# Moving the next batch's first scores and the up-projection heads by one chunk, and all whole down-projection blocks to Strassen, in an attention-plus-MLP kernel

## The chip, the cores and the metric

One core of a Trainium2 chip. The metric is the device time of one execution in microseconds (us). Kernels sent together run on the same chip, beside runs of the kernel before.

## The reference, cut to what matters

```python
# attention, batch 8, S = 3008, D = 256, d_qk = 64
attn = np.maximum(scale * (z @ z.T), 0.0) ** 2      # symmetric; no softmax
x    = u * (attn @ v)
# MLP over all 24064 tokens, d_ff = 2048
h = x @ w_in
g = h / (1 + np.exp(-1.702 * h))
out = g @ w_out
```

## The kernel before: the parts that matter

Each batch goes through six chunks of 512 query rows (the last has 448). TensorE (PE) does everything that is large. A *score unit* (two 64-row matmuls, a ReLU on ACT, a square on DVE) is taken ahead of the chunk that needs it, between attention matmuls ("hosted"). As the scores are symmetric, most units are also turned by a DMA transpose on SP's queue and used a second time (`tt`). Attention chunks run with the array as two 64-row halves; chunk 5, the up-projection and the Strassen products use the full array.

```python
def attend(b, i, both=False):
    ...
    half = [(0, TOP, NJ - 1), (1, LOW, NJ - 1)]           # the last 64 keys
    elif i == NCH - 1:                                     # full array: half block FIRST
        order = [half] + [[(c, FULL, j)] for c in cs for j in js]
    else:                                                  # 64-row halves, swapped in the middle
        order = [[(0, TOP, j), (1, LOW, j)] for j in js] + [half] + [[(1, TOP, j), (0, LOW, j)] for j in js]
    ...
    acc, turn = {}, NJ if order[-1][0][1] != FULL else -1
    def step(k):
        ...
            if k == turn:
                behind(acc["sig"], ins)                    # waits for the no-op
        if k == turn - 1:
            acc["sig"] = post(done)                        # sig = pool.nop(), after these matmuls
```

In the middle of a 64-row chunk the two halves swap accumulator banks, and `post`/`behind` keeps their order by a no-op on POOL: PE waits for POOL, POOL for PE.

```python
def load_w(k):                       # up weights W1 in 4 loads (2 MB of f32), down weights W2 in 4
    if k == 0:
        pool.tensor_copy(hold, XT[0, 1][:, 0, :1])
    if k < 4: pool.dma_start(W1[...], ...)
    else:     pool.dma_start(W2[...], ...)

LAGY = 2 * NFG + 4                   # up groups hosted by chunk 5: 20
NST = 4                              # blocks 0..3 by Strassen (7 products), the others:
def down64(b, k): ...                # 64-row halves, hosts the next batch's first 12 score units
# (chunk, step): which load; all in batch 0
LOADW = {(3, NJ + 1): 0, (3, NJ + 11): 1, (4, 2): 2, (4, 10): 3, (5, 0): 4, ...}
```

## Time and profile before

| | before |
|---|---|
| time, median | 1203.2 us (1201.6 to 1206.8, 4 runs) |
| span of the profiled run | 1200.5 us |
| least matmul time (below) | 1178.0 us |
| span above that | 22.5 us |

The page of the kernel before: busy time by engine, then the chain of waits.

```profile
PE 1189.5 (99%) x11775; PEld 720.5 (60%) x11775; DVE 828.1 (69%) x1273; ACT 766.4 (64%) x899; POOL 306.3 (26%) x363
...
PE 95%; DMA 2%; DVE 2%; ACT 1%; issue 0%; ACTq 0%
PE o L322 37%; PE hg L363 27%; PE st L463 18%; PE yp L529 8%; PE sc L226 6%; DMA tt<-a 2%; DVE a L254 1%; ACT rl L240 0%; PE w L97 0%; DVE gt L372 0%; DVE zst L122 0%; ACT gf L371 0%; DVE s L436 0%; DVE s L434 0%; DVE ZT L139 0%
```

So PE is the bound. Here `o` is attention, `hg` the up-projection, `st` a Strassen product, `yp` the plain down-projection, `sc` scores.

Windows of batch 1 (chunks 0 to 4; chunk 5 with up heads; up-projection with products; 64-row down):

```profile
core 0: us, PE busy (x) PEld busy (x) DVE busy (x) ACT busy (x) POOL busy (x), PEclk, DMA share, GB/s
165.70:223.30 57.60, 57.19 (x536) 29.75 (x532) 29.44 (x43) 29.50 (x34) 6.73 (x11) 1.00 0.90 155
223.30:250.40 27.10, 27.10 (x134) 12.73 (x131) 22.64 (x34) 20.47 (x20) 13.81 (x13) 1.00 0.46 69
250.40:299.50 49.10, 49.10 (x567) 36.06 (x567) 42.10 (x65) 33.00 (x44) 19.52 (x21) 1.00 0.44 127
299.50:313.40 13.90, 13.90 (x242) 11.53 (x240) 6.63 (x12) 10.42 (x13) 0.78 (x1) 1.00 0.72 150
```

PE idles 0.4 us in 147.7. The DMA engines are 90% busy in chunks 0 to 4 (the transposes).

The timeline of PE at the border from products to the 64-row down-projection, and inside it:

```profile
297.87 1.06 PE L463 MATMUL st<-W,s 128*128 128x128 f16 x16
298.86 0.50 PE L529 MATMUL yp<-W,gt 64*128 64x256 f16 x6
...
300.50 2.35 PE L529 MATMUL yp<-W,gt 64*128 64x256 f16 x40
302.69 0.59 PE L226 MATMUL sc<-ZT 64*128 64x512 f16 x4
```

Read starts, not durations, as matmuls overlap. Forty 64-row matmuls take 302.69 - 300.50 = 2.19 us, 55 ns each. Sixteen products at 55.9 ns would end at 298.76, but the next starts at 298.86: a change of array mode costs 0.10 us.

*Least matmul time.* In undisturbed stretches the spacing of full-array matmuls of N columns is N / 2.4 GHz + 2.5 ns (74 64-row attention matmuls of 512 columns, which run two at a time, take 7.99 us: 215.9 ns a pair; 240 products of 128 columns take 13.41 us: 55.9 ns each). The Trainium skill, "TensorE: Matmul & The Clock Gate", section "Wait — 56ns, not 53.3ns?", gives the same formula, and this trace agrees. I add it up over all matmuls of a stretch and call the rest *excess*.

Two more views, of batch 0, that the change will alter. PE's timeline, and the windows there:

```profile
58.06 0.38 PE L322 MATMUL o<-tt,V 64*128 64x512 f16 x2
58.88 1.04 PE L322 MATMUL o<-tt,V 64*128 64x512 f16 x8 [0.45 <-DMA tt<-a]
```

### The profile page before, as it was taken

The numbers are of one execution on the slowest core, as the hardware profiler recorded it, in microseconds if no ns is written. First come the engines' busy times: TensorE is split into PE (matmuls) and PEld (weight loads), VectorE is DVE, ScalarE is ACT, GpSimd is POOL, SyncE is SP. The second block draws the span as 40 slices with busy tenths as digits, with TensorE's granted clock in tenths as the row PEclk, the third lists the DMA queues.
The fourth block names the chain that finished last, engine by engine and source line by source line (L and its number), as shares of the span: only waits on it lengthen the run. The fifth ranks groups of instructions, "written<-read, shape, count | busy, mean of one in ns | idle before, by whom it ended". The sixth has DMA issues, their size and how long they took to land.

```text
span 1200.5 us, 28209 instructions
## 1 busy us (share of the span) xinstructions
PE 1189.5 (99%) x11775; PEld 720.5 (60%) x11775; DVE 828.1 (69%) x1273; ACT 766.4 (64%) x899; POOL 306.3 (26%) x363
## 2 busy tenths in 40 slices
PE   8999999999999999999999999999999999999998
PEld 3446765467654676546764468554775447855577
DVE  7659955597545976469654696638965489564886
ACT  6767684476844768367683676836677366772764
POOL 5144300352004520044200461015520145101000
PEclk9999999999999999999999999999999999999999
DMA  9987389562994639944399453984449854497012
GB/s 221 190 132 123 121 161 163 87 155 73 162 172 87 151 91 163 165 83 137 94 171 164 77 137 101 184 139 78 137 117 173 142 85 138 120 178 130 1 37 72
DMA packets 370816, 153.38 MB, mean 128 GB/s; under 512 B 317536, under 2 KB 362720, under 8 KB 370688
## 3 DMA queue, kind: packets, MB, share of 16 engines
q1 hardware_dynamic: 334400, 114.99, 49.6%
q0 software_dynamic: 35456, 35.86, 14.6%
q8 instruction: 92, 1.51, 0.5%
q10 hardware_dynamic: 832, 0.72, 0.2%
q14 instruction: 36, 0.29, 0.1%
HBM read 60.29 MB, written 24.64 MB: 71 GB/s over the span
## 4 chain that ended last, share of the span: by engine, by line
PE 95%; DMA 2%; DVE 2%; ACT 1%; issue 0%; ACTq 0%
PE o L322 37%; PE hg L363 27%; PE st L463 18%; PE yp L529 8%; PE sc L226 6%; DMA tt<-a 2%; DVE a L254 1%; ACT rl L240 0%; PE w L97 0%; DVE gt L372 0%; DVE zst L122 0%; ACT gf L371 0%; DVE s L436 0%; DVE s L434 0%; DVE ZT L139 0%
## 5 line engine op out<-in xcount | busy, mean ns | idle before, releaser
L371 ACT ACTIVATE gf<-hg 128x1024 f32<-128x1024 f32 (+1 forms) x384 | 385.8, 1006 | 167.3 <-PE hg L363 140.2
L240 ACT ACTIVATE rl<-sc 128x1024 f16<-128x1024 f32 x307 | 303.9, 1026 | 210.4 <-PE sc L226 208.3
L322 PEld LDWEIGHTS <-V 64*128 64x128 f16 (+1 forms) x4052 | 238.8, 94 | 246.1 <-issue 9.4
L363 PE MATMUL hg<-xt,W 128*128 128x512 f16 (+1 forms) x1408 | 354.6, 374 | 0.1
L372 DVE TENSOR_SCALAR gt<-gf 128x1024 f16<-128x1024 f32 (+1 forms) x384 | 275.8, 718 | 89.1 <-ACT gf L371 85.2
L254 DVE TENSOR_TENSOR a<-rl 128x1024 f16<-128x1024 f16 x272 | 190.0, 701 | 186.2 <-ACT rl L240 184.2
L322 PE MATMUL o<-a,V 64*128 64x512 f16 (+2 forms) x1982 | 313.3, 372 | 0.3 <-DVE a L254 0.3
L191 POOL DMA_DIRECT2D uq<-in_u_dram x188 | 129.4, 695 | 508.7 <-PE sc L226 342.3
L322 PE MATMUL o<-tt,V 64*128 64x512 f16 (+1 forms) x1790 | 218.2, 376 | 1.6 <-DMA tt<-a 1.3
L363 PEld LDWEIGHTS <-W 128*128 128x128 f16 x1536 | 141.2, 98 | 117.5 <-issue 0.3
L463 PEld LDWEIGHTS <-gt 128*128 128x128 f16 x2176 | 132.4, 98 | 28.7
L226 PE MATMUL sc<-ZT 64*128 64x512 f16 (+1 forms) x684 | 120.6, 366 | 4.2 <-DVE ZT L139 2.5
L463 PEld LDWEIGHTS <-s 128*128 128x128 f16 x1632 | 99.2, 98 | 20.7
L176 POOL CAST V<-vst 128x512 f16<-128x512 f32 x96 | 91.2, 986 | 64.2 <-DMA vst<-in_v_dram 64.0
L529 PE MATMUL yp<-W,gt 64*128 64x256 f16 x1664 | 104.0, 269 | 0.0
L529 PEld LDWEIGHTS <-gt 64*128 64x128 f16 x1664 | 80.4, 94 | 19.2 <-POOLq L85 4.1
L339 DVE TENSOR_TENSOR xt<-o,ut 128x512 f16<-128x512 f32 x80 | 51.5, 685 | 38.5 <-PE o L322 38.5
L463 PE MATMUL st<-WT,gt 128*128 128x128 f16 x1088 | 71.9, 219 | 0.0
L463 PE MATMUL st<-W,gt 128*128 128x128 f16 x1088 | 71.7, 219 | 0.0
L463 PE MATMUL st<-WT,s 128*128 128x128 f16 x1088 | 71.5, 219 | 0.0
L473 ACT ACTIVATE uP<-st 128x256 f32<-128x256 f32 x102 | 39.0, 382 | 35.7 <-DVE y L479 30.8
L226 PEld LDWEIGHTS <-ZT 64*128 64x128 f16 x684 | 37.9, 94 | 39.3 <-issue 7.8
(47 smaller groups left out, 626.5 us busy)
## 6 DMA issues: line engine op xcount, KB each, us to landing
vst<-in_v_dram SPq DMA_DIRECT2D x39, 512.0 KB, 5.0
uq<-in_u_dram POOLq DMA_DIRECT2D x156, 128.0 KB, 3.4
out_dram<-y SPq DMA_DIRECT2D x33, 512.0 KB, 3.8
tt<-a SPq DMA_TRANSPOSE x234, 3.4
uq<-in_u_dram POOLq DMA_DIRECT2D x32, 112.0 KB, 2.9
out_dram<-y POOLq DMA_DIRECT2D x7, 512.0 KB, 5.1
vst<-in_v_dram SPq DMA_DIRECT2D x8, 384.0 KB, 4.8
out_dram<-y POOLq DMA_DIRECT2D x7, 384.0 KB, 3.2
```

Source lines behind the costliest of these rows:

```text
L176: pool.tensor_copy(V16[b][:, n0:n0 + VB, k, :].rearrange("p n (q c) -> p n q c", c=QW), vst.rearrange("p n (q k c) -> p n q k c", k=NCC, c ...
L191: eng.dma_start(uq[k * QW:(k + 1) * QW, :n // QW].rearrange("t q k c -> t q (k c)"), src[:, :, cs])
L226: pe.matmul(sc[:, r, :m * P], zt[h, 2 * kp + r, :], zt[h, (qi + 1) * CB - m:(qi + 1) * CB, :], start=True, stop=True,)
L240: act.activation(rl, sc, AF.Relu, scale=csc)
L254: dve.tensor_tensor(a, rl, rl, ALU.mult)
L322: ins = pe.matmul(acc[c][:, :n], V16[b][h, j, c, :], weights(b, i, j)[h], start=(k, m) == first[c], stop=(k, m) == final[c],)
L339: dve.tensor_tensor(x[:, c, :n], acc[c][:, :n], ut[:, :n], ALU.mult)
L363: pe.matmul(hg[:, e, :n], W1[:, c, ff * P:(ff + 1) * P], XT[b, i][:, c, :n], start=(c == 0), stop=(c == NCC - 1),)
L371: act.activation(gf[:, :, :n], hg[:, :, :n], AF.Gelu_apprx_sigmoid, scale=1.0 / FSC)
L372: dve.tensor_scalar(g, gf[:, :, :n], FSC, None, ALU.mult)
L463: pe.matmul(bank[:, m, :], lhs()[:, f, m, :], right[:, ff, :], start=name in ("P1", "P2", "P5") and m == 0 and ff == 0, stop=ff == NFF // ...
L529: ins = pe.matmul(yp[s // per][:, s % per, :], GT[b, k, ff // CB][h, ff % CB, s * P:(s + 1) * P], W2[h, ff, :], start=new, stop=n == last[ ...
```

## The change

Intent: the 64-row down-projection goes; every whole block is done by Strassen (7 products instead of 8). Then something else must host the next batch's first score units: chunk 5 becomes a 64-row chunk and hosts ten of them. The up heads (18 groups now) move to chunk 4, which becomes a full-array chunk, except in the last batch. z of the next batch is loaded in chunk 4. After batch 0, V is cast by the DMA that loads it instead of on POOL, with the two channel halves interleaved, so that V's weight loads have stride 2. One scaling in four after the head moves to ACT. The core of the diff:

```diff
+    def full(b):
+        return NCH - 2 if b < B - 1 else NCH - 1
...
-        elif i == NCH - 1:
-            order = [half] + [[(c, FULL, j)] for c in cs for j in js]
+        elif i == full(b):
+            order = [[(c, FULL, j)] for c in cs for j in js]
+            order.insert(0 if i == NCH - 1 else len(order), half)     # chunk 4: half block LAST
...
-                    acc[c][:, :n], V16[b][h, j, c, :], weights(b, i, j)[h],
+                    acc[c][:, :n], V16[b][h, j].rearrange("p (c k) -> p k c", k=NCC)[:, c], weights(b, i, j)[h],
...
+        if q >= LAGY and q % 4 == 1:
+            act.activation(g, gf[:, :, :n], AF.Copy, scale=FSC)
+        else:
+            dve.tensor_scalar(g, gf[:, :, :n], FSC, None, ALU.mult)
...
-        return NST if b < B - 1 else NCH
+        return NCH - 1 + b % 2
...
-    def down64(b, k):  ...
+    def down(b, k, s):  ...                      # full array, only block 5 of even batches
-    LAGY = 2 * NFG + 4
+    LAGY = 2 * NFG + 2
...
-    LOADW = {(3, NJ + 1): 0, (3, NJ + 11): 1, (4, 2): 2, (4, 10): 3, (5, 0): 4, (5, 6): 5, (5, 12): 6, (5, 18): 7}
+    LOADW = {(2, NJ + 12): 0, (3, 4): 1, (3, 12): 2, (3, 20): 3, (4, 16): 4, (4, 22): 5, (4, 28): 6, (4, 34): 7}
...
+                if more and (i, n) == (NCH - 2, 2):
+                    load_z(b + 1)
```

Cut: larger buffer counts, the deferral of the next batch's transposes to the tail, new schedules of score units (`NEXT` for chunk 5), `load_u` and W1 in the interleaved channel order.

More of the change, by code (lines that the diff above doesn't have):

```diff
@@ L75 @@
     dve.memset(nil, 0.0)
-    late = []
+    late, LATE = [], []
     ZT, V16, UQ, UT, XT, unit, TT = {}, {}, {}, {}, {}, {}, {}
@@ L102, in first_z @@
             ZT[0] = pz.tile([P, NJ, P], F16, name="ZT", tag="ZT")
-            ZT["st"] = [pa.tile([P, CB * CB, 2, DQK], F16, name="zst", tag="tt", bufs=14) for _ in range(2)]
+            ZT["st"] = [pa.tile([P, CB * CB, 2, DQK], F16, name="zst", tag="tt", bufs=15) for _ in range(2)]
             ZT["f"] = [pw.tile([P, CB * CB, DQK], F32, name="zf", tag="y") for _ in range(2)]
@@ L148, in load_z @@
         for n0 in range(0, NJ, NU):
-            zst = pu.tile([P, NU, 2, DQK], F16, name="zst", tag="vst", bufs=3)
+            zst = pu.tile([P, NU, 2, DQK], F16, name="zst", tag="zst")
             full = min(NU, NJ - 1 - n0)
@@ L159, with load_v @@
     VB = 4
-    def load_v(b, n0, eng):
+    def load_v(b, n0):
         if n0 == 0:
-            V16[b] = pz.tile([P, NJ, NCC, P], F16, name="V16", tag="V16")
-        if b or n0 < 3 * VB:
-            vst = pu.tile([P, VB, D], F32, name="vst", tag="vst", bufs=3)
+            V16[b] = pz.tile([P, NJ, D], F16, name="V16", tag="V16")
+        if b:
+            dst, eng = V16[b][:, n0:n0 + VB], pool
         else:
-            vst = pa.tile([P, VB, D], F32, name="vst", tag="tt", bufs=14)
+            dst, eng = pa.tile([P, VB, D], F32, name="vst", tag="tt", bufs=15), sp if n0 else act
         full = min(VB, NJ - 1 - n0)
-        eng.dma_start(vst[:, :full, :], v[b, n0 * P:(n0 + full) * P].rearrange("(n p) c -> p n c", p=P))
+        eng.dma_start(dst[:, :full, :], v[b, n0 * P:(n0 + full) * P].rearrange("(n p) c -> p n c", p=P))
         if full < VB:
             for h in range(2):
-                eng.dma_start(vst[h * SREM:(h + 1) * SREM, full, :], v[b, S0:S])
-        for k in range(NCC):
-            pool.tensor_copy(
-                V16[b][:, n0:n0 + VB, k, :].rearrange("p n (q c) -> p n q c", c=QW),
-                vst.rearrange("p n (q k c) -> p n q k c", k=NCC, c=QW)[:, :, :, k, :],
-            )
+                eng.dma_start(dst[h * SREM:(h + 1) * SREM, full, :], v[b, S0:S])
+        if b == 0:
+            for n in range(0, VB, 2):
+                pool.tensor_copy(V16[b][:, n0 + n:n0 + n + 2], dst[:, n:n + 2])
     def width(i):
@@ L186, in load_u @@
         n = width(i)
-        uq = pu.tile([P, CH // QW, NCC, QW], F32, name="uq", tag="uq")
+        uq = pu.tile([P, CH // QW, QW, NCC], F32, name="uq", tag="uq")
         src = u[b, i * CH:i * CH + n].rearrange("(q t) c -> t q c", t=QW)
@@ L190, in load_u @@
             cs = slice(k * NCC * QW, (k + 1) * NCC * QW)
-            eng.dma_start(uq[k * QW:(k + 1) * QW, :n // QW].rearrange("t q k c -> t q (k c)"), src[:, :, cs])
+            eng.dma_start(uq[k * QW:(k + 1) * QW, :n // QW].rearrange("t q c k -> t q (c k)"), src[:, :, cs])
         UQ[b, i] = uq
@@ L197, in turn_u @@
         UT[b, i] = ut
-        dve.transpose(ut[:, :, :n // QW, :].rearrange("p k q t -> p q k t"), UQ.pop((b, i))[:, :n // QW])
+        dve.transpose(
+            ut[:, :, :n // QW, :].rearrange("p k q t -> p q k t"),
+            UQ.pop((b, i))[:, :n // QW].rearrange("p q c k -> p q k c"),
+        )
     def folded(b, i):
@@ L241, in square @@
         if folded(b, i) and jp == 2 * i:
-            a = pa.tile([P, CB, 2, P], F16, name="a", tag="a", bufs=21)
+            a = pa.tile([P, CB, 2, P], F16, name="a", tag="a", bufs=22)
             unit[b, i, jp] = a
@@ L245, in square @@
             dve.tensor_tensor(a.rearrange("p q r c -> p r q c"), r4, r4, ALU.mult)
-            unit[b, i, jp + 1] = pa.tile([P, 2, 2, CH // 2], F16, name="ad", tag="a", bufs=21)
+            unit[b, i, jp + 1] = pa.tile([P, 2, 2, CH // 2], F16, name="ad", tag="a", bufs=22)
             sp.dma_start_transpose(
@@ L251, in square, with turn_unit @@
             return
-        a = pa.tile([P, 2, CH], F16, name="a", tag="a", bufs=21)
+        a = pa.tile([P, 2, CH], F16, name="a", tag="a", bufs=22)
         unit[b, i, jp] = a
         dve.tensor_tensor(a, rl, rl, ALU.mult)
-        cj = jp // 2
-        if cj > i and (turned(b, i) or cj < NCH - 1):
-            if (b, i, cj) not in TT:
-                TT[b, i, cj] = pa.tile([P, CB, CB, P], F16, name="tt", tag="tt", bufs=14)
-            k0 = 2 * (jp % 2)
-            def turn_it():
-                sp.dma_start_transpose(
-                    TT[b, i, cj][:, k0:k0 + 2].rearrange("p r g c -> p (r g) c"),
-                    a.rearrange("p r c -> p (r c)"),
-                )
-            if b and i == 0 and 6 <= jp < NU - 2:
-                late.append(turn_it)
-                return
-            turn_it()
-            while late and (i, jp) == (1, NU - 1):
-                late.pop(0)()
+        if jp // 2 > i and (turned(b, i) or jp < NU - 2):
+            if b and i == 0 and LATE:
+                late.append(((jp + 2) % NU, lambda: turn_unit(b, i, jp, a)))
+            else:
+                turn_unit(b, i, jp, a)
+    def turn_unit(b, i, jp, a):
+        cj = jp // 2
+        if (b, i, cj) not in TT:
+            TT[b, i, cj] = pa.tile([P, CB, CB, P], F16, name="tt", tag="tt", bufs=15)
+        k0 = 2 * (jp % 2)
+        sp.dma_start_transpose(
+            TT[b, i, cj][:, k0:k0 + 2].rearrange("p r g c -> p (r g) c"),
+            a.rearrange("p r c -> p (r c)"),
+        )
     def weights(b, i, j):
@@ L367, in up_group @@
         if fg % 2 == 0:
-            GT[b, k, fg // 2] = pa.tile([P, CB, CH], F16, name="gt", tag="tt", bufs=14)
+            GT[b, k, fg // 2] = pa.tile([P, CB, CH], F16, name="gt", tag="tt", bufs=15)
         g = GT[b, k, fg // 2][:, (fg % 2) * FFG:(fg % 2 + 1) * FFG, :n]
@@ L371, in up_group @@
         act.activation(gf[:, :, :n], hg[:, :, :n], AF.Gelu_apprx_sigmoid, scale=1.0 / FSC)
-        dve.tensor_scalar(g, gf[:, :, :n], FSC, None, ALU.mult)
-        if SUMS:
-            SUMS.pop(0)()
+        if q >= LAGY and q % 4 == 1:
+            act.activation(g, gf[:, :, :n], AF.Copy, scale=FSC)
+        else:
+            dve.tensor_scalar(g, gf[:, :, :n], FSC, None, ALU.mult)
+        for s_ in [SUMS.pop(0) for _ in range(min(len(SUMS), 1 + (len(SUMS) > 8)))]:
+            s_()
         if k < nst(b) and fg == NFG - 1:
             SUMS.extend(left_sums(b, k) + (weight_sums() if b == k == 0 else []))
-    NST = 4
     def nst(b):
-        return NST if b < B - 1 else NCH
+        return NCH - 1 + b % 2
     SUMS, ST = [], {}
@@ L398, in load_w @@
         if k < 4:
-            w1v = moe_w_in.rearrange("(q k c) f -> q c k f", k=NCC, c=QW)
+            w1v = moe_w_in.rearrange("(q c k) f -> q c k f", k=NCC, c=QW)
             pool.dma_start(W1[k * QW:(k + 1) * QW], w1v[k])
@@ L431, in left_sum @@
             return
-        s_ = ST[b, k, name, h] = pa.tile([P, CB, 2, P], F16, name="s", tag="a", bufs=21)
+        s_ = ST[b, k, name, h] = pa.tile([P, CB, 2, P], F16, name="s", tag="a", bufs=22)
         if name == "S1":
@@ L510, in store, with down @@
                 )
-    def down64(b, k):
-        ns = blocks(b)[k][1] // P
-        shift, per = (2, 2) if ns == CB else (1, 1)
-        order = [(s, (s + shift) % ns, ff) for s in range(ns) for ff in range(NFF)]
-        turns = [32] if ns == CB else [16, 32]
-        last = {s // per: n for n, o in enumerate(order) for s in o[:2]}
-        yp, sigs = {}, {}
-        def step(n):
-            s0, s1, ff = order[n]
-            done = []
-            for s, h in ((s1, LOW), (s0, TOP)):
-                new = s // per not in yp
-                if new:
-                    yp[s // per] = ps1.tile([P, 2, D], F32, name="yp", tag="ps1")
-                ins = pe.matmul(
-                    yp[s // per][:, s % per, :], GT[b, k, ff // CB][h, ff % CB, s * P:(s + 1) * P], W2[h, ff, :],
-                    start=new, stop=n == last[s // per],
-                )
-                if n in turns:
-                    behind(sigs[n], ins)
-                done.append(ins)
-            if n + 1 in turns:
-                sigs[n + 1] = post(done)
-            for m in yp:
-                if n == last[m]:
-                    if (b, k) not in Y:
-                        Y[b, k] = pw.tile([P, CB, D], F32, name="y", tag="y")
-                    act.activation(Y[b, k][:, m * per:(m + 1) * per, :], yp[m][:, :per, :], AF.Copy, scale=1.0 / FSC)
-            if n == len(order) - 1:
-                store(b, k, pool)
-        return turns, [lambda n=n: step(n) for n in range(len(order))]
-    LAGY = 2 * NFG + 4
-    HEAD = 2
+    def down(b, k, s):
+        if s % 2 == 0:
+            ST[b, k, "yp"] = ps1.tile([P, 2, D], F32, name="yp", tag="ps1")
+        yp = ST[b, k, "yp"]
+        for ff in range(NFF):
+            pe.matmul(
+                yp[:, s % 2, :], GT[b, k, ff // CB][:, ff % CB, s * P:(s + 1) * P], W2[:, ff, :],
+                start=s % 2 == 0 and ff == 0, stop=ff == NFF - 1, skip_group_check=True,
+            )
+        last = s == blocks(b)[k][1] // P - 1
+        if s == 0:
+            Y[b, k] = pw.tile([P, CB, D], F32, name="y", tag="y")
+        if s % 2 or last:
+            act.activation(Y[b, k][:, s - s % 2:s + 1, :], yp[:, :s % 2 + 1, :], AF.Copy, scale=1.0 / FSC)
+        if last:
+            store(b, k, pool)
+    LAGY = 2 * NFG + 2
+    HEAD, HEAD0 = 2, 16
     def pieces(b, i):
@@ L559, in pieces @@
         return lst[:k] + lst[-2:] + lst[k:-2]
-    TAIL = {1: {n: 1 for n in (3, 12, 44, 54)}, 2: {n: 1 for n in (4, 25, 34, 43)}}
+    NEXT = {n: 1 for n in (4, 9, 14, 19, 29, 34, 39, 44)} | {NJ: 2}
     SCHED = {
@@ L565 @@
         2: {n: 1 for n in (2, 7, 12, 17)} | {NJ: 2},
-        3: {n: 1 for n in (14, 34)} | {NJ: 2},
-        4: {NJ: 2},
-        5: {},
+        3: {n: 1 for n in (6, 14, 32, 38)} | {NJ: 2},
+        4: {},
+        5: NEXT,
     }
+    SCHED_LAST = SCHED | {3: {n: 1 for n in (14, 34)} | {NJ: 2}, 4: {NJ: 2}, 5: {}}
     TURN0 = {(i, (38, 28)[i] if i < 2 else NJ + 4 if i < NCH - 1 else 12): i for i in range(NCH)}
@@ L575 @@
     TURN = {(1, NJ + 4): 2, (2, NJ + 4): 3, (4, NJ + 4): 4, (5, 8): 5}
-    LOADW = {(3, NJ + 1): 0, (3, NJ + 11): 1, (4, 2): 2, (4, 10): 3, (5, 0): 4, (5, 6): 5, (5, 12): 6, (5, 18): 7}
-    LOAD = {(3, NJ + 4): 4, (4, NJ + 5): 5}
+    LOADW = {(2, NJ + 12): 0, (3, 4): 1, (3, 12): 2, (3, 20): 3, (4, 16): 4, (4, 22): 5, (4, 28): 6, (4, 34): 7}
+    LOAD = {(3, NJ + 20): 4, (4, NJ + 5): 5}
     FIRST_ZT = {7: 3, 19: 4, 27: NCH - 1}
@@ L582 @@
         1: {0: 2, 8: 2, 15: 2, 22: 2, 30: 2, 38: 2},
-        2: {n: 1 for n in (0, 3, 7, 11, 30, 34, 38, 42)} | {NJ: 2},
-        3: {n: 1 for n in (4, 9, 14, 19)} | {NJ: 2},
-        4: {n: 1 for n in (4, 12, 20, 34)} | {NJ: 2},
-        5: {},
+        2: {n: 1 for n in (0, 3, 7, 11, 28, 32, 36, 40, 44)} | {NJ: 2},
+        3: {n: 1 for n in (3, 7, 11, 15, 19, 28, 32, 36, 40)} | {NJ: 2},
+        4: {},
+        5: NEXT,
     }
@@ L601 @@
     first_z(CB, 2 * CB, act)
-    load_v(0, 0, act)
+    load_v(0, 0)
     first_z(2 * CB, 4 * CB, sp)
     for n0 in (VB, 2 * VB):
-        load_v(0, n0, sp)
+        load_v(0, n0)
     first_z(4 * CB, NJ, sp)
     for n0 in range(3 * VB, NJ, VB):
-        load_v(0, n0, sp)
+        load_v(0, n0)
     warm_up(7)
@@ L625 @@
         nup = NCH * NFG
-        sched, turn, load = (SCHED, TURN, LOAD) if b else (SCHED0, TURN0, LOAD0)
-        head = 0
+        more = b + 1 < B
+        sched = SCHED0 if b == 0 else SCHED if more else SCHED_LAST
+        turn, load = (TURN, LOAD) if b else (TURN0, LOAD0)
+        head, first = 0, HEAD0 if b == 0 else HEAD
         for i in range(NCH):
+            host = b + 1 if more and i == NCH - 1 else b
+            if host > b:
+                fill(host)
+                LATE.append(host)
             for n, step in enumerate(attend(b, i, b == 0 and i < 2)):
@@ L641 @@
                     load_w(LOADW[i, n])
-                take(b, sched[i].get(n, 0))
-                if i == NCH - 1 and n >= HEAD and (n - HEAD) * LAGY // (2 * NJ - 2 - HEAD) >= head and head < LAGY:
+                if more and (i, n) == (NCH - 2, 2):
+                    load_z(b + 1)
+                take(host, sched[i].get(n, 0))
+                if i == full(b) and n >= first and (n - first) * LAGY // (2 * NJ - 2 - first) >= head and head < LAGY:
                     up_group(b, head)
@@ L646 @@
                 step()
-        more = b + 1 < B
         if more:
@@ L650 @@
                 load_u(b + 1, i)
-            load_z(b + 1)
             for n0 in range(0, NJ, VB):
-                load_v(b + 1, n0, sp)
-            fill(b + 1)
+                load_v(b + 1, n0)
         prods = products(nst(b))
@@ L662 @@
             product(b, *prods.pop(0))
-        for kp in prods:
-            product(b, *kp)
+        steps = [lambda kp=kp: product(b, *kp) for kp in prods]
+        if nst(b) < NCH:
+            k = NCH - 1
+            steps += [lambda s=s: down(b, k, s) for s in range(blocks(b)[k][1] // P)]
+        late.sort(key=lambda t: t[0])
+        for step in steps:
+            step()
             if SUMS:
                 SUMS.pop(0)()
+            for _, turn_it in [late.pop(0) for _ in range(min(len(late), 1 + (len(steps) < 10)))]:
+                turn_it()
+        LATE.clear()
         if more:
-            for k in range(NST, NCH):
-                turns, steps = down64(b, k)
-                at = {n: 3 - len(turns) for n in turns} | TAIL[len(turns)]
-                for n, step in enumerate(steps):
-                    take(b + 1, at.get(n, 0))
-                    step()
+            while late:
+                late.pop(0)[1]()
+            take(b + 1, 2)
 _INS = ['u', 'v', 'z', 'moe_w_in', 'moe_w_out']
```

## The prediction

> **What bounds the kernel now.** TensorE. The page's first part: PE busy 99% of 1200.5 us, clock 1.0. The chain of waits: 95% PE (attention 37%, up-projection 27%, Strassen products 18%, 64-row down-projection 8%, scores 6%). The waits view shows almost no PE idle. POOL (26%), ACT (64%), DVE (69%) are off the path. Windows of one batch (147.7 us): chunks 0-4 57.6, chunk 5 with up heads 27.1, up-projection with products 49.1, 64-row down 13.9. DMA is 90% busy in chunks 0-4 (transposes).
>
> **The change, costed.**
> 1. Down-projection. In the PE timeline 40 64-row matmuls advance 2.18 us: 54.5 ns each, 128 per whole block = 6.97 us. A Strassen block is 112 matmuls at 55.9 ns (240 in 13.41 us) = 6.25 us. Ten blocks switch (block 4 of seven batches, block 5 of batches 1, 3, 5): -7.2 us. Block 5 of even batches goes from 96 x 54.5 = 5.23 us to 48 full-array matmuls, estimated 109 ns each: no gain.
> 2. Scores, up groups and attention are moved, totals equal. Chunk 4 (full array) hosts 18 up groups; chunk 5 (64-row) ten score units of the next batch: two more mode changes per batch. The Trainium skill, "TensorEngine Tiling (Array Packing)", Key Properties, says a mode change drains the array; here each costs about 0.1 us of start-to-start time. 7 x 2 x 0.1 = +1.5 us.
> 3. In chunk 5 each score unit needs 1026 ns of ACT and gets five attention pairs (0.95 us) plus its own 0.22 us: just enough. Attention tiles are tight (12 for chunk 5, 8 sums, 10 new in 22): estimated 0 to 0.5 us per batch.
> 4. Deferred transposes pile up in the short tail (about 10 us): eight at 2 us each. Chunk 1 may wait: 0 to 1 us per batch.
> 5. V's POOL casts (986 ns each) mostly go; V's weight loads become stride-2. "TensorE: Matmul & The Clock Gate", Weight-path perf modes, allows strided columns for the fast load; no run shows it yet. Loads take 94-98 ns against 189-216 ns per attention slot; even doubled they should hide. Worth nothing.
> 6. DVE gets the sums of ten more Strassen blocks (8 x 0.75 us each), loses eight output scalings a batch to ACT; both have room.
>
> **Sum.** -7.2 + 1.5, perhaps -1 from stalls that vanish and +1 to +2 from new ones: about -6 us.
>
> **Predicted: 1197.5 us, 8 in 10 between 1188 and 1209. Faster by over 2%: 0.04; within 2%: 0.92; slower by over 2%: 0.04.**
>
> **What would show each step.** (1) The 64-row down group gone, products up from 3808 to 4928 at the same spacing, a small full-array down group; batches 0.7 to 1.4 us shorter. (2) About 0.1 us extra at the borders of chunks 4 and 5. (3) PE idle for ACT rl in chunk 5. (4) PE idle for transposed tiles in chunks 0-1. (5) V's weight load near 95 ns, or longer with attention still at 216 ns per pair. (6) No PE hg waits in chunk 4.
>
> **What would make it wrong.** Stride-2 loads so slow that attention's spacing grows (an estimated 471 us of the span is attention columns: 10% is 47 us). Transposed z or V late for chunk 5 or chunk 0. Transposes starving chunk 1. DVE behind in chunk 4 (scaling plus sum 1.48 us per group against about 1.4 us of PE). On the other side, stalls that I took as unavoidable going away.

## More of the kernel before

```profile
core 0: us, PE busy (x) PEld busy (x) DVE busy (x) ACT busy (x) POOL busy (x), PEclk, DMA share, GB/s
57.00:62.00 5.00, 4.55 (x44) 1.93 (x42) 2.50 (x4) 3.83 (x4) 0.73 (x2) 1.00 1.39 183
62.00:67.00 5.00, 5.00 (x50) 2.26 (x48) 3.14 (x4) 0.68 (x2) 2.71 (x5) 1.00 0.93 180
72.00:82.00 10.00, 10.00 (x73) 4.88 (x69) 5.98 (x9) 6.67 (x7) 5.39 (x8) 1.00 1.15 168
```

I read a DMA share over 1 as packets that wait for one another: these stretches are the fullest of the kernel. Yet PE waits only 0.45 us for a transposed tile. The eight weight loads here (W1's four and the first four of W2), by the view of tile W:

```profile
DMA to landing us min/median/max: 4.5/5.4/7.6
```

## The result

| | before | after |
|---|---|---|
| time, median | 1203.2 us | 1220.8 us (1220.6 to 1221.4, 4 runs) |
| ratio | | 1.0143 (95%: 1.012 to 1.0166) |
| span | 1200.5 us | 1218.8 us |
| least matmul time | 1178.0 us | 1170.6 us |
| span above that | 22.5 us | 48.2 us |
| mean granted clock | 1.000 | 0.995 |

Ratios are the mean time of one kernel's fast runs over that of the other's in the same rounds, so not quite the ratio of the medians quoted.

The kernel became slower, and the range 1188 to 1209 missed. But the least matmul time fell by 7.3 us, as predicted (7.2). The gain was there and was more than lost. Where, by batch and chunk (excess in us, from the starts of PE's matmuls in the trace; about 5.3 us of start-up, the same in both kernels, are left out of batch 0):

| excess, us | chunks 0-1 | 2 | 3 | 4 | 5 | up | tail | sum |
|---|---|---|---|---|---|---|---|---|
| batch 0 before | 6.7 | 0.0 | 0.6 | 0.2 | 0.4 | 0.0 | 0.3 | 8.1 |
| batch 0 after | 6.7 | 0.2 | 5.5 | 11.7 | 0.8 | 0.0 | 0.2 | 25.2 |
| batches 1-6 before, mean | 0.2 | 0.2 | 0.0 | 0.2 | 0.1 | 0.0 | 0.2 | 0.85 |
| batches 1-6 after, mean | 0.5 | 0.0 | 0.1 | 0.6 | 0.6 | 0.0 | 0.4 | 2.2 |

Balance: -7.3 (matmul time) + 17.1 (batch 0) + 8.1 (batches 1 to 6) + 0.5 (batch 7) = +18.3 us, the difference of the spans (the parts are rounded).

Page of the changed kernel, the same lines:

```profile
PE 1192.4 (98%) x11423; PEld 721.2 (59%) x11423; DVE 826.9 (68%) x1327; ACT 821.9 (67%) x971; POOL 231.3 (19%) x325
...
PE 85%; DMA 4%; DVE 3%; issue 3%; ACT 2%; POOL 2%; POOLq 0%; ACTq 0%; DVEq 0%
```

"98% busy" hardly moved, yet 48 us lie above the least time: a PE at half clock counts as busy, and short waits vanish in the modelled ends of matmuls. The chain of waits is the better sign: PE's part fell from 95% to 85%.

Windows of batch 1 (chunks 0 to 3; chunk 4; chunk 5; up-projection with products; tail), to be read against the four rows before:

```profile
182.10:229.20 47.10, 47.03 (x438) 24.61 (x434) 27.00 (x40) 29.88 (x33) 4.41 (x6) 1.00 0.96 174
229.20:255.50 26.30, 25.75 (x120) 11.38 (x118) 18.92 (x28) 17.69 (x18) 8.46 (x9) 1.00 0.69 82
255.50:267.30 11.80, 11.62 (x118) 5.97 (x118) 9.56 (x16) 9.67 (x11) 5.13 (x8) 1.00 0.35 80
267.30:319.00 51.70, 51.70 (x586) 37.64 (x585) 39.36 (x66) 41.53 (x54) 11.52 (x16) 1.00 0.43 88
319.00:331.30 12.30, 12.01 (x212) 11.69 (x211) 9.66 (x18) 3.85 (x9) 0.16 (x1) 1.00 0.91 160
```

PE now idles in chunk 4 (0.55 us), chunk 5 and the tail, where it did not before.

The tail of batch 0 (`yp` is now the small full-array form): 48 matmuls in 5.23 us after 0.10 us for the mode change at the end, 109 ns each, as estimated.

```profile
176.31 5.40 PE L524 MATMUL yp<-W,gt 128*128 128x256 f16 x48
181.64 0.61 PE L228 MATMUL sc<-ZT 64*128 64x512 f16 x4
```

Now batch 0. PE's timeline, chunks 3 and 4:

```profile
58.70 0.39 PE L326 MATMUL o<-tt,V 64*128 64x512 f16 x2
62.62 1.04 PE L326 MATMUL o<-tt,V 64*128 64x512 f16 x8 [3.53 <-DMA tt<-a]
63.50 0.66 PE L228 MATMUL sc<-ZT 64*128 64x512 f16 x4
63.94 1.92 PE L326 MATMUL o<-a,V 64*128 64x512 f16 x8
65.65 0.64 PE L228 MATMUL sc<-ZT 64*128 64x512 f16 x2
...
81.92 1.01 PE L326 MATMUL o<-tt,V 128*128 128x512 f16 x2 [5.89 <-DMA tt<-a]
...
89.77 0.38 PE L326 MATMUL o<-a,V 128*128 128x512 f16 x1
92.28 0.39 PE L326 MATMUL o<-a,V 128*128 128x512 f16 x1 [2.13 <-POOLq L85]
```

Three waits, two for transposed tiles and one for POOL's no-op (line 85 is `pool.nop()`). After the first, eight matmuls that should take 0.86 us start to start take 1.71 (63.94 to 65.65). The windows show why:

```profile
57.00:62.00 5.00, 2.10 (x20) 0.88 (x16) 2.51 (x4) 2.83 (x3) 0.00 (x0) 1.00 1.37 126
62.00:67.00 5.00, 4.38 (x28) 1.76 (x30) 1.80 (x3) 2.61 (x3) 0.00 (x0) 0.69 1.03 138
72.00:82.00 10.00, 4.11 (x20) 1.82 (x19) 1.78 (x3) 1.48 (x2) 0.00 (x0) 0.95 1.66 113
82.00:92.00 10.00, 8.15 (x24) 2.88 (x23) 3.06 (x4) 4.09 (x4) 4.37 (x6) 0.71 0.79 93
```

The column PEclk falls to 0.69 and 0.71. The trace's clock records give half clock for 3.41 us from 63.9 and for 6.83 us from 81.0. The Trainium skill, "TensorE: Matmul & The Clock Gate", Part 1, says that about 3.4 us without matmuls brings the clock to half, in free-running windows of 3413 ns. The durations agree, one and two such windows. The threshold does not. I marked off windows of 3.413 us from the clock records of all 13 traces and counted in each how long PE was idle. Leaving out the first 12 us and the last 4, every fall came at the end of a window with 1.96 us or more of idle time (2.13 us before the fall at 63.9), and no window with 1.70 us or less was followed by one; in the first 12 us, 1.4 to 1.5 us was enough in e3, e6 and e9. The wait of 2.1 us that ends at 92.28 did no harm: it lay across the border of two windows at 91.2, with 1.1 us in each. So the place of a wait counts as well as its length. The two long waits here cost an estimated 1.7 and 2.9 us on top of themselves, half of the time that PE then worked at half clock.

Why were the tiles late? W1's four loads in this kernel, the same view as before:

```profile
DMA to landing us min/median/max: 13.5/17.2/18.0
```

And the transposes around them, listed from the trace:

```
                    kernel before                        changed kernel
             issued    landed                     issued    landed
transpose     52.87     58.84  transpose           52.44     62.58
transpose     54.73     59.67  W1, first of four   54.07     67.53
transpose     57.68     62.56  transpose           54.20     76.07
transpose     59.05     63.53  W1, last of four    55.56     73.59
transpose     60.43     66.14  transpose           57.59     81.88
W1, first     60.59     65.13  next batch's z      70.56     83.15
W1, the rest  66.8-67.9 71.5-74.0
```

W1's 2 MB now leave POOL as one burst at 54 us, into the busiest stretch of the kernel. In the program the four loads stand at separate steps from the end of chunk 2 to the middle of chunk 3, but no no-op of POOL's queue stands between them: the trace has the no-op of chunk 2 at 47.05 and that of chunk 3 at 63.70, behind the burst. In the kernel before they stood behind the no-op of chunk 3, which ran at 59.97, and three of them also behind a load of u (64.29 to 66.80). In e2 below, put behind that no-op again, they leave at 61.3. POOL's timeline, the changed kernel first, then the kernel before:

```profile
54.07 1.99 POOL L405 DMA_DIRECT2D W<-in_moe_w_in_dram  x4
```

```profile
60.59 0.54 POOL L400 DMA_DIRECT2D W<-in_moe_w_in_dram  x1 [0.29 <-issue]
```

The transpose issued at 54.20 then takes 22 us to land instead of 5. The Trainium skill, "DMA: Bandwidth & Descriptors", Queues, rings and completion order, says that each DMA engine takes turns between its queues packet by packet; the landings fit that (both queues make progress, both slowly), but no run here shows the order of packets. Sharing alone does not explain it: from 66 to 74 us the DMA engines moved 46 GB/s at a share of 1.26, where the kernel before moved 152 GB/s at 0.82. Why loads and transposes slow one another that much stays open.

The third wait has another source. POOL's timeline in the changed kernel:

```profile
83.97 1.08 POOL L152 DMA_DIRECT2D zst<-in_z_dram  x1
85.05 1.49 POOL L155 DMA_DIRECT2D zst<-in_z_dram  x2
90.96 0.83 POOL L156 COPY zst<-zst 128x768 f16<-128x768 f16 x1 [4.42 <-DMA zst<-in_z_dram]
```

`load_z` puts a copy on POOL that waits for z. PE goes on at 92.28, just after that copy (90.96 + 0.83 = 91.79). The no-op of chunk 4 stands behind the copy; its record is at 92.21. And chunk 4 needs no such no-op. The line `turn = NJ if order[-1][0][1] != FULL else -1` recognises a 64-row chunk by its last step; the change put the half block last in the full-array chunk 4, so the test came out wrong, and a full-array chunk got a half-way synchronisation through POOL. The Trainium skill, "TensorE: Matmul & The Clock Gate", table of specifications, calls GpSimdE's queue strictly first-in first-out; the trace agrees, as the no-op (92.21) comes after the copy that stands before it (90.96).

In batches 1, 3 and 5 the same no-op costs 0.7, 0.9 and 1.05 us, in batch 4 0.2 and in batches 2 and 6 nothing. The trace shows why: it runs 14.5, 13.2, 14.7, 13.9, 14.8 and 13.2 us after the first attention matmul of chunk 4 in batches 1 to 6, and what it costs is what exceeds 13.75 us. In batches 1 to 5 it runs within 0.2 us of the landing of the last z load, so a later z is a longer wait.

### The profile page after: what moved, and what is told of

Read it like the earlier page. It is cut to its first block, busy times and chain, and to the rows that moved or that the text cites. A ratio compares the mean times of both kernels' runs of the same rounds, so it can differ in the third digit from the quotient of the medians.

```text
span 1218.8 us, 27565 instructions
## 1 busy us (share of the span) xinstructions
PE 1192.4 (98%) x11423; PEld 721.2 (59%) x11423; DVE 826.9 (68%) x1327; ACT 821.9 (67%) x971; POOL 231.3 (19%) x325
## 4 chain that ended last, share of the span: by engine, by line
PE 85%; DMA 4%; DVE 3%; issue 3%; ACT 2%; POOL 2%; POOLq 0%; ACTq 0%; DVEq 0%
PE o L326 34%; PE hg L367 22%; PE st L468 21%; PE sc L228 6%; DMA zst<-in_z_dram 3%; PE yp L524 2%; DMA tt<-a 1%; ACT rl L242 1%; DVE a L256 1%; DVE gt L379 1%; ACT gf L375 1%; POOL uq L190 1%; POOL zst L152 1%; DMA ZT<-zst 1%; POOL zst L156 0%
## 5 line engine op out<-in xcount | busy, mean ns | idle before, releaser
L379 DVE TENSOR_SCALAR gt<-gf 128x1024 f16<-128x1024 f32 (+1 forms) x328 | 230.8, 704 | 149.3 <-ACT gf L375 147.4
L326 PE MATMUL o<-a,V 64*128 64x512 f16 (+3 forms) x2272 | 302.9, 369 | 2.5 <-POOLq L85 2.1
L326 PE MATMUL o<-tt,V 64*128 64x512 f16 (+1 forms) x1524 | 236.3, 378 | 11.9 <-DMA tt<-a 9.7
L468 PEld LDWEIGHTS <-gt 128*128 128x128 f16 x2816 | 169.5, 98 | 32.2 <-issue 1.6
L468 PEld LDWEIGHTS <-s 128*128 128x128 f16 x2112 | 127.2, 98 | 22.8
L468 PE MATMUL st<-WT,gt 128*128 128x128 f16 x1408 | 92.9, 219 | 1.1 <-ACT uP L478 1.1
L468 PE MATMUL st<-W,gt 128*128 128x128 f16 x1408 | 92.3, 219 | 0.0
L468 PE MATMUL st<-WT,s 128*128 128x128 f16 x1408 | 91.0, 219 | 0.0
L484 DVE SCALAR_TENSOR_TENSOR y<-st,uP 128x256 f32<-128x256 f32 x132 | 55.5, 420 | 29.4 <-ACT uP L478 18.3
L443 DVE TENSOR_TENSOR s<-gt,s 128x1024 f16<-128x1024 f16 x88 | 59.8, 683 | 0.0
L441 DVE TENSOR_TENSOR s<-s,gt 128x1024 f16<-128x1024 f16 x88 | 59.6, 682 | 0.0
```

What stands on the lines that cost most here:

```text
L326: ins = pe.matmul(acc[c][:, :n], V16[b][h, j].rearrange("p (c k) -> p k c", k=NCC)[:, c], weights(b, i, j)[h], start=(k, m) == first[c], s ...
L379: dve.tensor_scalar(g, gf[:, :, :n], FSC, None, ALU.mult)
L441: dve.tensor_tensor(s_, ST[b, k, "S1", h], a11, ALU.subtract)
L443: dve.tensor_tensor(s_, a12, ST[b, k, "S2", h], ALU.subtract)
L468: pe.matmul(bank[:, m, :], lhs()[:, f, m, :], right[:, ff, :], start=name in ("P1", "P2", "P5") and m == 0 and ff == 0, stop=ff == NFF // ...
L484: dve.scalar_tensor_tensor(y[:, :, o, c], ST[b, k, "bank" + x], 1.0 / FSC, ST[b, k, "after" + u_], ALU.mult, ALU.add,)
```

## The experiments

Theory A: the loss has two main causes in batch 0, W1's early burst (transposes starved, then half clock) and the stray no-op behind z's copy, and small waits in each later batch. Rival: the denser score schedule of batch 0 (11 units in chunk 3 instead of 6) needs more transposes than the queue can turn.

The first four ran on one chip; the kernel before took 1206.6 us there (7 runs).

### e1: without the stray synchronisation

```diff
-        acc, turn = {}, NJ if order[-1][0][1] != FULL else -1
+        acc, turn = {}, NJ if not both and i != full(b) else -1
```

> The changed kernel, with the half-way synchronisation of chunk 4 taken out (a full-array chunk needs none; it is only set because the half block stands last there). Theory A (this sync is a no-op in POOL's queue and waits behind the copy of the next batch's z): the PE waits put down to POOLq vanish, 2.3 us in batch 0 and 0.7, 0.9, 1.05 us in batches 1, 3, 5; time 1220.8 - 5 = about 1216. Rival (something else holds PE there, for example accumulator banks): the same waits come back under another name, time within 1 us of 1220.8.

Measured: 1212.3 us (1208.7 to 1221.5), ratio 1.0055 (1.0008 to 1.0102); span 1209.5. All POOLq waits in chunk 4 are gone: batches 1 to 6 have 0.12 us of excess in chunk 4. But batch 0's chunk 4 still has 9.4 us: W1's burst still starves the transposes (landings up to 23 us after issue), with waits of 2.1 and 2.6 us, each followed by 3.41 us of half clock. The no-op is confirmed as the cause of its wait; the total is not compared with the changed kernel here, as that ran on another chip (e11 below, the changed kernel on a third chip, has a ratio of 1.006, so the times of e1 and e2 alone show no gain).

### e2: W1 behind the middle of chunk 3

```diff
-    LOADW = {(2, NJ + 12): 0, (3, 4): 1, (3, 12): 2, (3, 20): 3, (4, 16): 4, ...
+    LOADW = {(3, NJ): 0, (3, NJ + 1): 1, (3, NJ + 2): 2, (3, NJ + 3): 3, (4, 16): 4, ...
```

> The changed kernel, with the four loads of the up-projection weights placed behind the middle of chunk 3 of batch 0, about where the kernel before has them, instead of from the end of chunk 2 on. Theory A (these 2 MB, issued as one burst at 54 us, fill the DMA engines, and the transposed tiles that PE needs land up to 20 us late, after which PE runs at half clock): the 3.7 and 6.05 us waits and the 5 us lost at half clock go; batch 0 shrinks by about 14 us; time about 1207. Rival (the denser score schedule of batch 0 makes more transposes than the queue can turn): the waits stay, time within 3 us of 1220.8.

Measured: 1213.5 us, ratio 1.0048 (1.0016 to 1.008); span 1213.9. The expected time was missed by 7 us, yet the waits for transposes did shrink to 0.6 and 0.9 us, and W1 lands in 6.7 to 9.2 us (PE waits 1.6 us for W1 itself). Instead PE runs into the stray no-op, which grew; with 10.24 us at half clock around it, chunk 4 has 13.2 us of excess, against 11.7 in the changed kernel. PE's timeline of this run, then POOL's:

```profile
78.92 0.38 PE L326 MATMUL o<-a,V 128*128 128x512 f16 x1
86.48 0.61 PE L326 MATMUL o<-a,V 128*128 128x512 f16 x1 [7.18 <-POOLq L85]
```

```profile
85.16 0.83 POOL L156 COPY zst<-zst 128x768 f16<-128x768 f16 x1 [4.74 <-DMA zst<-in_z_dram]
```

PE reached the no-op 11 us earlier than in the changed kernel (78.9 against 89.8), but z had landed only 6 us earlier. Removing one wait handed the time to the next one in line.

### e3: both edits

> The changed kernel with both of the edits before. Theory A: the two add up, 1220.8 - 14 - 5 = about 1202, and batch 0 has at most 9 us over its ideal matmul time (25 us in the changed kernel, 8 in the kernel before). Rival (denser schedule): above 1212.

Measured: 1204.5 us (1201.9 to 1208.1), ratio 0.9981 (0.9951 to 1.0011); span 1201.0. Batch 0 has 10.4 us of excess, where at most 9 were expected; its chunk 3 fell to 0.3 and chunk 4 to 0.55 us, and 1.7 us are left in chunk 5. W1 lands in 4.1 to 6.5 us:

```profile
DMA to landing us min/median/max: 4.1/5.3/6.5
```

The score schedule is as dense as in the changed kernel, and the waits are gone: the rival falls as their main cause. It is not cleared altogether, as e7 and e10 below had waits for transposed tiles in batch 0 with W1 late. Alone the two edits left ratios of 1.0055 and 1.0048; together they give 0.9981, clear of the changed kernel's 1.006 (e11) and 1.0143. They sit one behind the other.

### e4: the kernel before, with W1 early

```diff
-    LOADW = {(3, NJ + 1): 0, (3, NJ + 11): 1, (4, 2): 2, (4, 10): 3, (5, 0): 4, ...
+    LOADW = {(2, NJ + 12): 0, (3, 4): 1, (3, 12): 2, (3, 20): 3, (5, 0): 4, ...
```

> The kernel before, with nothing changed but the position of the four loads of the up-projection weights: from the end of chunk 2 on, as the changed kernel has them. Theory A: the transposes of chunks 2 and 3 of batch 0 are starved here too, one or two PE waits of 3 to 6 us with half clock after them; time 1203 + 5 to 14 = 1208 to 1217. Rival (the schedule of scores is the cause, not the weights): time within 2 us of 1203.

Measured: 1218.2 us (1216.9 to 1221.2) against 1206.6, ratio 1.0096 (1.007 to 1.0121). W1 takes 11.8 to 16.3 us to land, and PE stands still in chunk 3, far longer than the 3 to 6 us expected, with 13.65 us at half clock from 62.1:

```profile
57.11 0.38 PE L322 MATMUL o<-tt,V 64*128 64x512 f16 x2
70.88 1.46 PE L322 MATMUL o<-tt,V 64*128 64x512 f16 x6 [13.39 <-DMA tt<-a]
```

Four numbers in a schedule, with everything else of the old kernel in place, cost 1%. This shows that the early burst is enough by itself, without the denser scores.

### e5 to e8: the small waits (another chip; before 1205.3 us, 7 runs)

After e3, batches 1 to 6 still have 1.7 us of excess on average, 0.9 us more than before. Three waits recur: 0.45 us in the tail of odd batches (ACT), 0.36 us in chunk 5 (ACT, behind DVE), twice 0.2 us in chunk 0 (ACT). In chunk 5 DVE waits for PE to free an attention tile; DVE's timeline in the changed kernel:

```profile
260.30 0.38 DVE L240 TENSOR_TENSOR ad<-rl 128x512 f16<-128x512 f16 x1
262.26 1.90 DVE L256 TENSOR_TENSOR a<-rl 128x1024 f16<-128x1024 f16 x3 [1.59 <-PE o L326]
```

**e5**, e3 with all scaling on DVE:

```diff
-        if q >= LAGY and q % 4 == 1:
-            act.activation(g, gf[:, :, :n], AF.Copy, scale=FSC)
-        else:
-            dve.tensor_scalar(g, gf[:, :, :n], FSC, None, ALU.mult)
+        dve.tensor_scalar(g, gf[:, :, :n], FSC, None, ALU.mult)
```

> The kernel with both repairs (e3), and all scaling of the up-projection's output on DVE again, as in the kernel before, instead of one in four on ACT. Theory: the 0.45 us wait of PE for an ACT copy of a product, in the tail of batches 1, 3, 5 and 7, comes from the scalings that ACT now does (1.06 us each, in order before that copy); without them it goes, time 1.8 us shorter than e3 (about 1202.5 where e3 had 1204.5), nothing else moves. Rival (the shorter head of 18 up groups causes it): the wait stays.

Measured: 1200.0 us (1199.3 to 1205.2), ratio 0.9975 (0.9937 to 1.0013); span 1197.5. The tail's excess in odd batches fell from 0.55 to 0.11 us in batches 3 and 5, to 0.25 in batch 1, and by 0.5 us in batch 7. The ACT scalings were the cause. The ratio does not resolve the 1.8 us that were expected (e3 had 0.9981).

**e6**, e3 with 16 heads:

```diff
-    LAGY = 2 * NFG + 2
+    LAGY = 2 * NFG
```

> e3 with 16 up groups in chunk 4 instead of 18, so that two Strassen sums fewer hold attention tiles in chunk 5. Theory (in chunk 5 the third square finds no free tile and waits until PE has read an old one; scores back up behind it): the DVE wait for PE (1.6 us) in chunk 5 goes, and with it the 0.36 us wait of PE in six batches and most of the 1.6 us in batch 0; about 3 us shorter than e3. Rival (chunk 5 is simply short of ACT time): the PE waits stay.

Measured: 1209.4 us, ratio 1.0032 (1.0001 to 1.0063): a miss, though the interval overlaps that of e3. The mechanism was right: chunk 5's excess fell from 0.58 to 0.23 us. But two more products now run beside the up-projection, so in odd batches the last block's products come too early for their sums. Three new waits of 0.7 us each by the starts appear there (DVE), 2.2 us of excess per odd tail. PE's timeline, which shows 0.50 us of the first as idle:

```profile
309.01 0.40 PE L468 MATMUL st<-WT,s 128*128 128x128 f16 x4 [0.50 <-DVE s L441]
```

**e7**, e3 with evenly spaced scores:

```diff
-        0: {n: 1 for n in (4, 8, 12, 16, 20, 28, 32, 36, 40, 44)} | {NJ: 2},
-        1: {n: 1 for n in (2, 7, 12, 17)} | {NJ: 2},
+        0: {n: 1 for n in range(5, 46, 4)},
+        1: {n: 1 for n in (2, 7, 12, 17, 21)} | {NJ: 2},
```

> e3 with the twelve score units of chunk 0 taken one at a time every fourth step from the fifth on (the last of them in chunk 1), instead of from the fourth step with two at once in the middle. Theory: two waits of 0.2 us each per batch for ACT in chunk 0 go, 0.4 x 7 = 2.8 us shorter than e3; chunk 1 waits for transposes no more than before. If the order of the transposes matters more than ACT, waits for transposed tiles in chunk 1 or 2 appear.

Measured: 1211.2 us, ratio 1.0048 (1.0004 to 1.0091): slower, a miss. Chunk 0 gained only 0.12 us: without the double score unit in the middle, the half-way no-op itself shows, 0.28 us. The double unit was there to cover it. Chunk 1 has 0.4 to 0.8 us in batches 1 to 6, as its unit at step 21 crowds the double one at 24 (0.42 us) and transposes are later. Batch 0, whose chunk 0 and 1 the edit does not touch, had a 5.9 us wait for a transposed tile in chunk 2 of the profiled run; two of the four runs lay at 1214 us with clock 0.997 and two at 1205 to 1208 with 1.000. Batch 0 is on the edge by itself.

**e8**, e3 with all three:

> e3 with the three edits of e5, e6 and e7 together. If the three waits are separate they add up: about 1.8 + 3 + 2.8 = 7 us shorter than e3, so about 9 us (0.7%) under the kernel before in the same rounds, which is the 7.3 us of matmul time that the change takes away plus a little. If they hide one another, less than 4 us under e3.

Measured: 1209.9 us, ratio 1.005 (1.0003 to 1.0098). This is a miss too: 7 us less than e3 were expected. The waits did add up in the trace, but with e6's and e7's new ones among them: chunk 5 at 0.23 us, tails of odd batches at 2.1 us, chunk 1 at 0.4. The two slowest runs (1213 and 1217 us, clock 0.997 and 0.996) were not profiled.

### e9 to e11: a version that keeps the covers (a third chip; before 1206.1 us, 11 runs)

**e9**, e5 with shifted score units:

```diff
-    NEXT = {n: 1 for n in (4, 9, 14, 19, 29, 34, 39, 44)} | {NJ: 2}
+    NEXT = {n: 1 for n in (4, 9, 14, 19, 30, 35, 40, 45)} | {NJ: 2}
-        0: {n: 1 for n in (4, 8, 12, 16, 20, 28, 32, 36, 40, 44)} | {NJ: 2},
-        1: {n: 1 for n in (2, 7, 12, 17)} | {NJ: 2},
+        0: {n: 1 for n in (6, 10, 14, 18, 29, 33, 37, 41, 45)} | {NJ: 2},
+        1: {n: 1 for n in (2, 7, 12, 17, 30)} | {NJ: 2},
```

> e5 with the score units shifted: in chunk 5 the last four one step later (30, 35, 40, 45), so that the backlog behind the third square is gone when they come; in chunk 0 the first one at step 6 instead of 4, no unit in the six steps before the double one, one unit moved to chunk 1 behind its middle. The double unit in the middle stays: it hides the half-way no-op of POOL, 0.28 us, as e7 showed. Theory: the 0.36 us wait in chunk 5 and one or both of the 0.2 us waits in chunk 0 go, 3 to 5 us shorter than e5, profile span about 1193 to 1195. Rival (as in e6 and e7, a wait taken away there comes back as a wait for transposes in chunk 1, or as a wait at the chunk's end): within 1.5 us of e5.

Measured: 1200.0 us (1197.5 to 1203.0, 6 runs) against 1206.1, ratio 0.9952 (0.9931 to 0.9973); span 1196.0. Chunk 0's excess in batches 1 to 7 went from 0.41 to 0.00 us, chunk 5's from 0.58 to 0.39. Part came back, as the rival said: waits of 0.5 to 0.8 us in chunk 1 in four of six batches (in batch 1 the trace shows it as a wait for a transposed tile). Of the 3 to 5 us hoped for, the spans of the profiled runs show 1.5 (1196.0 against 1197.5 in e5); the medians against e10, on the same chip, show 3.0, but the two intervals overlap.

**e10**, the kernel of e5 again:

> The kernel of e5 unchanged, with five rounds, beside e9 and the kernel before: is the repaired change faster than the kernel before? From the traces (span 1197.5 against 1200.5) about 3 us or 0.25% faster, so a ratio of 0.997 to 0.998; if the ratio's interval takes in 1, the two are the same for this chip's noise.

Measured: 1203.1 us (1199.7 to 1207.8, 6 runs), ratio 0.9973 (0.995 to 0.9996). The profiled run was a bad one (span 1206.0): a 2.0 us wait for a transposed tile and a 3.3 us wait for ACT, both in batch 0.

**e11**, the changed kernel again:

> The changed kernel again, on the chip of these rounds, so that the repaired kernels are compared with it and not with another day's numbers. Expected: 1.2 to 1.6% over the kernel before, and the same two starved waits in batch 0, though their sizes may differ by some us, as batch 0 runs with its DMA engines full.

Measured: 1212.3 us (1211.3 to 1218.2, 4 runs), ratio 1.006 (1.0034 to 1.0086): less than expected. In the profiled run batch 0 had 19.1 us of excess instead of 25.2: 1.7 us waiting for a transposed tile and 6.8 us at the no-op, plus half clock. The landings are late here too (transposes up to 15.7 us, W1 8.8 to 11.9 us), but only one tile wait is left and the no-op has taken over most of the loss.

| kernel | ratio to before | 95% |
|---|---|---|
| changed (result above; e11) | 1.0143; 1.006 | 1.012-1.0166; 1.0034-1.0086 |
| e3, both repairs | 0.9981 | 0.9951-1.0011 |
| e5 and e10, also DVE scaling | 0.9975; 0.9973 | 0.9937-1.0013; 0.995-0.9996 |
| e9, also shifted scores | 0.9952 | 0.9931-0.9973 |

## Why the prediction was wrong

The mechanism of the gain was right, and the term for new stalls was mis-sized. Point by point, by the prediction's own numbers:

1. *Down-projection, -7.2 us.* Right: least matmul time fell by 7.3 us, at unchanged spacings (55.9 ns per product, 109 ns in the small form).
2. *Two more mode changes per batch, +1.5 us.* Right: each border of chunks 4 and 5 shows 0.10 to 0.12 us.
3. *Chunk 5's score units, 0 to 0.5 us per batch.* Right in mechanism and at the upper end: 0.36 us for the freed tile plus 0.12 us for the double unit. e6 confirmed the tile. A wait of the same kind in chunk 0 (0.2 us, the two units taken at the end of the tail) was not foreseen.
4. *Transposes piling up in the tail, 0 to 1 us in chunk 1.* Almost absent: 0.17 us in batch 3, 0.46 us in batch 6, nothing in the others.
5. *Stride-2 weight loads worth nothing.* Right: V's 64-row load has a mean of 94 ns before and after, and attention keeps 216 ns a pair. The POOL casts were off the path, as said.
6. *DVE and ACT have room.* Wrong in a small thing: there was room on average, but one ACT scaling just ahead of a product's copy cost 0.45 us per odd batch (e5).

The step that failed is the sum's last part, "+1 to +2 from new ones". New stalls cost about 24 us: 17.1 in batch 0 and 8.1 in batches 1 to 6, less the 1.5 us counted as mode changes. Read from the trace, about 14 of them follow W1's burst (waits of 3.7 and 6.05 us by the starts, and an estimated 4.6 at half clock), about 5 the stray no-op (2.3 in batch 0, 2.9 in batches 1 to 5), and most of the rest are the small waits in chunks 0 and 5. I read the schedule tables for score units closely, but passed over the lines that moved the weight loads and `load_z`. My list of risks had transposed tiles starving chunk 1 and late z; what starved were chunks 3 and 4 of batch 0, by W1. The trace of the kernel before held the warning: a DMA share of 1.39 in 57-62 us, with a wait of 0.45 us already there. And the stray no-op was readable in the diff: `order[-1]` was a proxy for "64-row chunk", and the diff changed the order.

What stays open: why z lands later in some batches than in others, why loads and transposes slow one another as they do, and what decides in which of its waits batch 0 loses its time from run to run. W1 is not the only source of late transposes: two that were issued at 53 and 55 us in e2, before W1 left at 61.3, took 10.7 and 10.8 us, and in e7 one issued at 32 us took 12.5.

## What to carry to other kernels

Work out for each moved load what will really hold it back: its place in the program means nothing where its queue has no wait, and a synchronisation standing ahead of it may have been its only brake. When a repair gives nothing, look in the trace whether its wait is gone and the next one in line has grown, and try both repairs together before dropping either. Conditions that infer a mode from a detail (`order[-1]`) should name the mode, as the next change will move the detail.

## What the Trainium skill lacked or had wrong

- "TensorE: Matmul & The Clock Gate", Back-to-back issue gap, gives for streams of weight load and matmul a sustained 81 ns at N = 128 and 131 ns at N = 512. Here such streams, with one weight load per matmul, ran at 55.9 and 216 ns, which is the page's formula for the isolated gap.
- The same page, LDWEIGHTS, gives P / 1.2, which is 107 ns for 128 columns; the trace shows 98 ns (94 ns for a 64-row load), and 94 ns as well with columns at stride 2. Whether a fast load was on, the trace does not tell.
- The same page, Part 1, asks for an idle window of about 3.4 us before the clock halves; idle times of 2.1 us (e1) and 2.0 us (e10) were followed by 3.41 us at half clock. In these traces, after start-up, 1.96 us of idle time within one window of 3.413 us was enough and 1.70 us was not.
- "TensorEngine Tiling (Array Packing)" says that a mode change drains the array but not what that costs: 0.10 to 0.12 us here.
- "DMA: Bandwidth & Descriptors" has no figure for transposes beside a burst of loads from another queue: landing went from 4-6 us to as much as 24 us under 2 MB of weight loads, and those from 5 to 17 us.
- No page says what a POOL no-op used as a relay between two PE matmuls costs: 0.28 us where nothing covers it (e7).
